# Sink scores of four head pairs in four 32-column tiles, one exp per block, and sink values spread by a mask product

## The chip, the core and the metric

The program runs on one NeuronCore of a Trainium2 chip. The core has five engines with instruction queues of their own: TensorE (PE, matrix products, with weight loads listed apart as PEld), VectorE (DVE), ScalarE (ACT), GpSimd (POOL) and SyncE (SP, used here only to issue transfers). Matrix products land in PSUM, eight banks of 128 partitions; everything else lives in SBUF. The metric is the device time of one execution in microseconds (us). Lower is better.

## What is computed

Attention with a sliding window and sink tokens, followed by a two-layer MLP. There are 4 batches, 8 heads, 768 tokens and a head dimension of 64.

```python
keep = (pos_k < 4) | ((pos_q - pos_k >= 0) & (pos_q - pos_k < 128))
a = softmax(where(keep, q @ k.T / 8, -1e9))
x = (a @ v).transpose(0, 2, 1, 3).reshape(3072, 512)
h = x @ w_in                          # 512 -> 2048
out = (h * sigmoid(1.702 * h)) @ w_out   # 2048 -> 512
```

So each query sees the 128 tokens up to its own, and the first four tokens of its batch: the sinks. For queries in the first 256 tokens of a batch the kernel treats the sinks with the window itself. For all later queries the sinks are scored apart.

## The kernel before

Work is cut into 12 blocks of 256 tokens, three for each batch (`NK = B * R`; the block is `k`, its batch `b`, its place in the batch `r`). The eight heads are handled as four pairs `p`; two heads of 64 fill 128 partitions. For every block the kernel does this:

- **load** (L375): q, k and v of the block come from memory as float32, by SP (two of block 0 by ACT). GpSimd, VectorE or ScalarE cast them to float16 (`copy`, L277-278; every cast has that line).
- **turn** (L472): q and k are transposed to `blkT`, by PE for the first four blocks (`turn_on_pe`, transposes at L507, the permutation `perm` as second operand) and by a transposing DMA for the rest.
- **sink keys and values**, only for the first block of a batch. GpSimd copies the four sink keys out of the transposed block into `ks16` (L493). It is a matrix of 128 columns for each pair, zero outside the sink columns. GpSimd copies the sink values into `vs16` (L455) in four small copies. Both tensors are set to zero once, at the start, on GpSimd (L329, L330).
- **front** (L537), for blocks with `r > 0`, once for each pair: one 128x128 product of the sink keys with the 256 queries (L547) into a bank of PSUM, and one exp on ScalarE into `ats` (L555). With 8 such blocks these are 32 products and 32 exps. Only 8 of the 128 output rows of a pair belong to sinks; the rest multiply zero rows of `vs16` later.
- **scores** (L559): window scores for one pair or two, in products of 64 rows of the array each, the two heads of a pair in the two halves (L589), exp on ScalarE (L609), and from block 2 on a mask product on VectorE (L616). Blocks 0 and 1 add the mask as a bias on PE instead (L582).
- **back** (L627): attention times values on PE (L649), sinks among them, a reciprocal (L667), a normalising product (L669) and a transpose to `xT` (L688 on PE for blocks 0 to 2, by DMA later).
- **mm1** (L702) and **mm2** (L734): the MLP, L716 and L745, with tanh on ScalarE (L728) and a product on VectorE (L730) between. The result is scaled and copied to `osb` (L764, L766) and written out (L775). All writes go through SP's queue except the very last, a piece of 64 rows by 128 columns, which goes through ScalarE's.

The order of instructions on each engine isn't written by hand. A planner (`Plan.run`, L68) takes every step as an operation with an assumed duration on its engine, its dependencies, a priority that plays the part of a due time, and what it needs of PSUM (`acq`, seven banks shared by classes such as "k" for sink scores and "s" for window scores). It simulates the engines and lists the operations in the order in which they would start. It also puts products of zeros (`warm`, L823) on PE wherever PE would be idle in the first 12 us of its own clock. What comes out is a fixed order for each engine: an instruction that waits holds up everything behind it on its engine. Weights (`weights`, L342) are issued by GpSimd, in the same queue as its casts and copies.

Of the kernel before, what the change touches and what calls it, by code (L numbers as in the profile page):

```python
# [26 lines left out]
def _build_constants() -> np.ndarray:  # L27

    t = _token_of()
    rel = t[None, :] - t[:, None]  # L30
    return np.concatenate([np.eye(P), rel <= 0, rel > 0], axis=1).astype(np.float16)


class Op:
# [18 lines left out]
class Plan:  # L53
# [4 lines left out]
    def op(self, eng, dur, lat, fn, deps=(), prio=0.0, acq=None, rel=(), kind=""):  # L58
        return self.any({eng: (dur, lat)}, lambda _: fn(), deps, prio, acq, rel, kind)
# [130 lines left out]
def pe_ns(n):  # L190
    return n / 2.4 + 2.5
# [3 lines left out]
def kernel(  # L195
# [34 lines left out]
    def ring(name, n, shape, dt):  # L230
        return [pool.tile(list(shape), dt, name=f"{name}{i}") for i in range(n)]

    const = pool.tile([P, 3 * P], FP16, name="const")
    ident = const[:, 0:P]
    seen = pool.tile([P, 2 * P], FP16, name="seen")
    perm = pool.tile([P, P], FP16, name="perm")
# [4 lines left out]
    w_out16 = pool.tile([P, NF, d_model], FP16, name="w_out16")  # L241
    blkT = ring("blkT", RB, (P, 2, NP, 2, P), FP16)
    vs16 = pool.tile([P, B, NP, 2, E], FP16, name="vs16")
    ks16 = pool.tile([P, B * NP, P], FP16, name="ks16")
    qk32 = ring("qk32", RS, (P, 2, H, 2, D), FP32)
    v32 = ring("v32", RS, (P, H, 2, D), FP32)
    qk16 = ring("qk16", RQ, (P, 2, 2, H, D), FP16)
    v16 = ring("v16", RV, (P, 2, H, E), FP16)
    at = ring("at", RA, (P, 2, 512), FP16)
    ats = ring("ats", RA, (P, TB), FP16)  # L250
    rcp = ring("rcp", RR, (P, 2, 2), FP32)
    xn = ring("xn", RR, (P, 2, 2, D), FP16)
    xb = ring("xb", 2, (P, 2, NP, 2, D), FP16)
# [34 lines left out]


    NEVER = -1e9  # L290
    o_zero = op("DVE", 100, 200, lambda: nc.vector.memset(zero, 0.0), prio=NEVER, kind="const")  # L291
    o_ident = op("POOL", 700, (300, 8), lambda: nc.gpsimd.dma_start(const, const_d.ap()), prio=NEVER - 1, kind="load")

# [18 lines left out]
    def biases():  # L312
# [13 lines left out]
    o_perm = op("POOL", 330, 450, lambda: nc.gpsimd.tensor_copy(  # L326
        out=perm.rearrange("r (h g) -> r h g", h=NP), in_=ident.rearrange("r (g h) -> r h g", h=NP)),
        [o_ident], prio=NEVER, kind="const")
    o_vs0 = op("POOL", 2200, 2300, lambda: nc.gpsimd.memset(vs16, 0.0), prio=NEVER + 3, kind="const")  # L329
    o_ks0 = op("POOL", 2200, 2300, lambda: nc.gpsimd.memset(ks16, 0.0), prio=NEVER + 2, kind="const")  # L330
    o_table = op("ACT", 1300, 1400, lambda: nc.scalar.activation(out=dummy, in_=zero[:, 0:8], func=AF.Exp),
                 [o_zero], prio=NEVER + 8, kind="const")

# [41 lines left out]
    def load(k):  # L375
# [74 lines left out]
                o_cv[k, p] = got  # L450
        if r == 0:
            def f():
                for t in range(2):
                    for i in range(2):
                        nc.gpsimd.tensor_copy(  # L455
                            out=vs16[64 * t + 32 * i : 64 * t + 32 * i + 2, b, :, i],
                            in_=w16[64 * t : 64 * t + 2, 0, i::2],
                        )
            o_vs[b] = op("POOL", 1400, 1500, f, [*o_cv[k, 0], *o_cv[k, NP - 1], o_vs0], prio=nominal(k - 1, 0), kind="vs")
            uses("v16", k % RV, o_vs[b])  # L460

    k_ap = k

# [8 lines left out]
    def turn(k):  # L472

        b, r = divmod(k, R)
        h8 = L / 8
        base = attend(k, 0)
        c16, T = qk16[k % RQ], blkT[k % RB]
        war = reuse("blkT", k % RB)
        o_t = []
        if k < KT:  # L480
            for i in range(2):
                for e in range(2):
                    o_t.append(turn_on_pe(k, e, i, T, eights(c16)[:, e, i], war))
        else:
            o_t.append(turn_by_dma(k, T, slots(c16), war))
        for p in range(NP):
            o_qkT[k, p] = [o[p] for o in o_t]
        o_t = list({id(o): o for x in o_t for o in x}.values())
        if r == 0:
            def ks():  # L490
                for i in range(2):
                    d = slice(64 * i, 64 * i + 64)
                    nc.gpsimd.tensor_copy(  # L493
                        out=ks16[d, NP * b : NP * b + NP].rearrange("d p (i a) -> d p i a", i=2)[:, :, :, 32 * i : 32 * i + 2],
                        in_=T[d, 1, :, 0].rearrange("d p (i a) -> d p i a", i=2)[:, :, :, 0:2],
                    )
            o = op("POOL", 500, 640, ks, o_t + [o_ks0], prio=base - 4 * h8, kind="ks")
            uses("blkT", k % RB, o)
            for p in range(NP):
                o_ks[b, p] = o  # L500
# [33 lines left out]
        uses("qk16", k % RQ, o)  # L534
        return [o] * NP

    def front(k, p):  # L537

        b, r = divmod(k, R)
        u = NP * k + p  # L540
        base = attend(k, 2 * p)
        h8 = L / 8
        Q = turned(k, p, 0)
        As = ats[u % RA]
        if r:
            def sk():
                nc.tensor.matmul(  # L547
                    f32(o_k)[:, 0:TB], ks16[:, NP * b + p], Q.rearrange("d j s -> d (j s)"),
                    start=True, stop=True,
                )  # L550
            war = reuse("ats", u % RA)
            o_k = op("PE", pe_ns(TB), TB / 2.4 + 166, sk, o_qkT[k, p] + [o_ks[b, p]] + war, prio=base - 3.1 * h8,
                     acq=("k", 1), kind="sink")
            hold(k, p, o_k)
            o_se[k, p] = op("ACT", TB / 1.2 + 50, TB / 1.2 + 170, lambda: nc.scalar.activation(  # L555
                out=As, in_=f32(o_k)[:, 0:TB], func=AF.Exp, scale=scale),
                [o_k] + war, prio=base - 2.6 * h8, rel=[(o_k, 0)], kind="exps")

    def scores(k, pairs):  # L559

# [66 lines left out]
    def back(k, p):  # L627
# [2 lines left out]
        u = NP * k + p  # L630
        base = attend(k, 2 * p)
        h8 = L / 8
        A, As = at[u % RA], ats[u % RA]
        vt, vp = v16[k % RV], v16[(k - 1) % RV]

        def avp():
# [12 lines left out]
                        nc.tensor.matmul(avp()[:, j, i], a_, v_, start=(n == 0), stop=(n == len(mms) - 1))  # L649

        dur = 12 * 31 if r else 6 * 31
        deps = [*o_m[k, p], *o_cv[k, p]] + ([o_se[k, p], *o_cv[k - 1, p], o_vs[b]] if r else [])
        rc, X = rcp[u % RR], xn[u % RR]
        if k < KX:
            war = reuse("xn", u % RR)
# [5 lines left out]
        o_a = op("PE", dur, dur + 166, av, deps + war, prio=base - 1.5 * h8, acq=("a", 1), kind="av")  # L661
        uses("at", u % RA, o_a)
        if r:
            uses("ats", u % RA, o_a)
            uses("v16", (k - 1) % RV, o_a)
        uses("v16", k % RV, o_a)
        o_r = op("DVE", 100, 200, lambda: nc.vector.reciprocal(out=rc, in_=avp()[:, :, :, D]),  # L667
# [66 lines left out]
    def mm2(k):  # L734
        b, r = divmod(k, R)
        g = gT[k % RG]
        for j, c0, c1 in ((0, 0, 512), (1, 0, 512)) if k < NK - 1 else ((0, 0, 512), (1, 0, 384), (1, 384, 512)):
            w = c1 - c0
            last = w < d_model
            holder = []  # L740
            prev = None
            for s in range(NS):
                def f(s=s, j=j, holder=holder, c0=c0, c1=c1, w=w):
                    for Fi in (2 * s, 2 * s + 1):
                        nc.tensor.matmul(  # L745
                            f32(holder[0])[:, 0:w], g[:, Fi, bass.ts(j, P)], w_out16[:, Fi, c0:c1],
                            start=(Fi == 0), stop=(Fi == NF - 1),
                        )
                deps = [o_g[k, s], o_w[4 + s // 2]] + ([prev] if prev else [])
                o = op("PE", 2 * pe_ns(w), pe_ns(w) + w / 2.4 + 166, f, deps,  # L750
                       prio=nominal(k + 1, 4 * j + s / 2) + 3 + c0 / 100 * L, acq=None if s else ("o", 1), kind="mm2")
                uses("gT", k % RG, o)
                holder.append(o)
                prev = o
            if not c0:
                oi = n_o[0] % RO
                n_o[0] += 1
                war = reuse("osb", oi)
            O = osb[oi]
            row = k * TB + j * P  # L760

            def f(e, O=O, holder=holder, c0=c0, c1=c1, w=w):
                if e == "ACT":
                    nc.scalar.mul(O[:, c0:c1], f32(holder[0])[:, 0:w], 0.5)  # L764
                else:
                    nc.vector.tensor_scalar_mul(O[:, c0:c1], f32(holder[0])[:, 0:w], 0.5)  # L766

            prio = nominal(k + 1, 4 * j + 4) + 4
            e = "DVE" if c0 else "ACT"
            o_c = [op(e, w / 1.2 + 50, w / 1.2 + 170, lambda f=f, e=e: f(e), [holder[-1]] + war, prio=prio,  # L770
                      rel=[(holder[0], 0)], kind="oc")]
            for i in range(2):
                eng = "ACT" if c0 and i else "SP"
                def f(O=O, i=i, row=row, c0=c0, c1=c1, dma=nc.scalar if eng == "ACT" else nc.sync):
                    dma.dma_start(  # L775
                        out[row : row + P, c0:c1].rearrange("(p i) f -> i p f", i=2)[i], O[64 * i : 64 * i + 64, c0:c1]
                    )
                o_d = op(eng, 590, (420, 4), f, o_c, prio=prio, kind="out")
                uses("osb", oi, o_d)
# [3 lines left out]
    for k_ in range(NK):  # L783
        load(k_)
        turn(k_)
        for p_ in range(NP):
            front(k_, p_)
        for ps_ in [(0,), (1,), (2,), (3,)] if k_ < PAIRED_FROM else [(0, 1), (2, 3)]:
            scores(k_, ps_)
        for p_ in range(NP):  # L790
            back(k_, p_)
        if k_ >= 1:
            mm1(k_ - 1)
        if k_ >= 2:
            mm2(k_ - 2)
# [79 lines left out]
```

## Time and profile before

Four runs took 224.36 to 225.09 us, with a median of 224.85 us. The profiled execution took 224.98 us, of which the instructions span 223.0 us.

| engine | busy, us | share of the span | instructions |
|---|---|---|---|
| PE | 217.7 | 98% | 2186 |
| ACT | 132.9 | 60% | 263 |
| DVE | 125.0 | 56% | 272 |
| POOL | 90.7 | 41% | 158 |

A matrix product's listed duration includes its way through the array, during which the next one already runs: 768 products at L716 have a mean of 273 ns, while eight of them in a row take 0.87 us on the chain of waits, or 109 ns each. So the space that a product takes on PE is read from the chain or from the starts of neighbours, not from its mean duration. The granted clock of PE is full in all of the span.

### The profile page before, as it was taken

To read this page: it belongs to the slowest core of one execution; us is meant where nothing else is said; L and a number is where in the kernel's file an instruction comes from. 1 tells how busy PE (TensorE), PEld (TensorE's weight loads), DVE (VectorE), ACT (ScalarE), POOL (GpSimd) and SP (SyncE) were. 2 spreads that over 40 slices of the span, in tenths; PEclk is the share of its full clock that TensorE was granted. 3 is DMA by queue.
4 is the path that set the end of the run, shared out by engine and by line. 5 is a ranking of instruction groups with operands and counts; after the bars stand their busy time and mean duration, and the time that the engine had idled before them with its cause. 6 is when DMAs were issued, how large, how long until landed. Compare 5 with 4: busy or idle time off the path is not lost.

```text
span 223.0 us, 5479 instructions
## 1 busy us (share of the span) xinstructions
PE 217.7 (98%) x2186; PEld 154.3 (69%) x2186; DVE 125.0 (56%) x272; ACT 132.9 (60%) x263; POOL 90.7 (41%) x158
## 2 busy tenths in 40 slices
PE   8999999999999999999999999999999999999993
PEld 8968977667757766766676667767667676666652
DVE  1675865588727765665555665575465655634310
ACT  3298555776557776565486577555577486444320
POOL 8299013578991785703815917507500000000000
PEclk9999999999999999999999999999999999999999
DMA  5999999999789989299599589399541212231224
GB/s 203 342 155 200 197 257 249 344 288 265 158 122 215 247 161 310 50 166 259 114 210 247 72 193 255 74 205 243 104 92 43 61 36 47 51 69 25 50 47 94
DMA packets 65864, 36.36 MB, mean 163 GB/s; under 512 B 27792, under 2 KB 60832, under 8 KB 65840
## 3 DMA queue, kind: packets, MB, share of 16 engines
q1 hardware_dynamic: 61200, 31.17, 59.1%
q0 software_dynamic: 4272, 4.29, 11.9%
q10 hardware_dynamic: 368, 0.56, 0.8%
q8 instruction: 17, 0.28, 0.5%
q14 instruction: 7, 0.06, 0.1%
HBM read 27.36 MB, written 6.29 MB: 151 GB/s over the span
## 4 chain that ended last, share of the span: by engine, by line
PE 93%; ACT 3%; DMA 1%; DVE 1%; issue 0%; SPq 0%; ACTq 0%
PE bank L716 38%; PE bank L745 35%; PE bank L649 6%; PE bank L589 5%; PE bank L823 4%; PE bank L547 2%; ACT at L609 1%; PE bank L507 1%; DMA out_dram<-osb 1%; PE bank L688 1%; PE bank L582 1%; ACT blkT L278 0%; DVE gT L730 0%; ACT osb L764 0%; ACT th L728 0%
## 5 line engine op out<-in xcount | busy, mean ns | idle before, releaser
L745 PE MATMUL bank<-w_out,gT 128*128 128x512 f16 (+2 forms) x400 | 100.2, 370 | 0.0
L716 PE MATMUL bank<-xT,w_in 128*128 128x256 f16 x768 | 100.1, 273 | 0.0
L730 DVE SCALAR_TENSOR_TENSOR gT<-th,bank 128x512 f16<-128x512 f16 x96 | 65.8, 685 | 48.5 <-ACT th L728 47.7
L716 PEld LDWEIGHTS <-w_in 128*128 128x128 f16 x768 | 72.9, 98 | 22.6 <-issue 2.5
L728 ACT ACTIVATE th<-bank 128x512 f16<-128x512 f32 x96 | 57.8, 602 | 46.1 <-PE bank L716 45.2
L278 POOL CAST qk<-qk 64x512 f16<-64x512 f32 (+1 forms) x73 | 44.3, 609 | 54.6 <-DMA qk<-in_q_dram 34.4
L609 ACT ACTIVATE at<-bank 128x512 f16<-128x512 f32 (+1 forms) x96 | 50.3, 571 | 14.7 <-PE bank L589 14.4
L745 PEld LDWEIGHTS <-gT 128*128 128x128 f16 x400 | 36.4, 98 | 21.9 <-issue 0.3
L616 DVE TENSOR_TENSOR at<-at,bank 128x1024 f16<-128x1024 f16 (+1 forms) x40 | 25.6, 640 | 20.7 <-ACT at L609 20.5
L278 POOL CAST v<-v 64x512 f16<-64x512 f32 x45 | 27.6, 614 | 6.4 <-DMA v<-in_v_dram 4.1
L649 PE MATMUL bank<-v,at 128*128 128x65 f16 x352 | 21.2, 193 | 0.2 <-DVE v L278 0.2
L764 ACT ACTIVATE osb<-bank 128x512 f32<-128x512 f32 (+1 forms) x24 | 14.4, 598 | 10.6 <-PE bank L745 10.6
L649 PEld LDWEIGHTS <-at 128*128 128x128 f16 x352 | 17.6, 98 | 4.0 <-issue 0.3
L555 ACT ACTIVATE ats<-bank 128x256 f16<-128x256 f32 x32 | 12.6, 394 | 7.1 <-PE bank L547 7.0
L669 DVE TENSOR_TENSOR xb<-bank,rcp 128x256 f16<-128x256 f32 x36 | 15.2, 421 | 0.5
L649 PE MATMUL bank<-vs,ats 128*128 128x65 f16 x128 | 14.8, 193 | 0.0
L667 DVE RECIPROCAL rcp<-bank 128x4 f32<-128x4 f32 x48 | 8.6, 179 | 9.5 <-PE bank L649 8.4
L649 PEld LDWEIGHTS <-ats 128*128 128x128 f16 x128 | 11.9, 97 | 2.2 <-ACT th L728 0.2
L589 PE MATMUL bank<-blkT 64*128 64x256 f16 x192 | 13.4, 244 | 0.0
L589 PEld LDWEIGHTS <-blkT 64*128 64x128 f16 x256 | 8.0, 94 | 7.7 <-issue 6.7
L823 PE MATMUL bank<-zero 128*128 128x128 f16 x99 | 8.6, 265 | 1.0 <-DVE zero L291 1.0
L547 PE MATMUL bank<-blkT,ks 128*128 128x256 f16 x32 | 8.7, 272 | 0.1
(41 smaller groups left out, 86.7 us busy)
## 6 DMA issues: line engine op xcount, KB each, us to landing
v<-in_v_dram SPq DMA_DIRECT2D x12, 512.0 KB, 7.0
out_dram<-osb SPq DMA_DIRECT2D x46, 128.0 KB, 2.7
qk<-in_q_dram SPq DMA_DIRECT2D x8, 512.0 KB, 5.1
qk<-in_k_dram SPq DMA_DIRECT2D x8, 512.0 KB, 6.1
qk<-in_q_dram SPq DMA_DIRECT2D x8, 256.0 KB, 5.1
w_in<-in_moe_w_in_dram POOLq DMA_DIRECT2D x4, 512.0 KB, 6.9
w_out<-in_moe_w_out_dram POOLq DMA_DIRECT2D x4, 512.0 KB, 14.4
qk<-in_k_dram SPq DMA_DIRECT2D x6, 256.0 KB, 5.5
```

The source lines that it names most:

```text
L278: {"POOL": nc.gpsimd.tensor_copy, "DVE": nc.vector.tensor_copy, "ACT": nc.scalar.copy}[e](out=out, in_=in_)
L589: nc.tensor.matmul(f32(o_s, 2 * n + i)[:, c : c + w], src[d, j], Q[d].rearrange("d j s -> d (j s)")[:, q0 : q0 + w], start=k >= KM, stop=T ...
L609: nc.scalar.activation(out=A[:, i, 0:W], in_=f32(o_s, 2 * n + i)[:, 0:W], func=AF.Exp, scale=scale)
L616: nc.vector.tensor_tensor(out=A[:, :, 0:W], in0=A[:, :, 0:W], in1=mask[:, c0 : c0 + W].unsqueeze(1).to_broadcast((P, 2, W)), op=ALU.mult,)
L649: nc.tensor.matmul(avp()[:, j, i], a_, v_, start=(n == 0), stop=(n == len(mms) - 1))
L669: o_n = op("DVE", 300, 425, lambda: nc.vector.tensor_tensor(out=X, in0=avp()[:, :, :, 0:D], in1=rc.to_broadcast((P, 2, 2, D)), op=ALU.mult ...
L716: nc.tensor.matmul(f32(holder[0])[:, bass.ts(e, TB)], w_in16[:, c, bass.ts(Fi, P)], X[:, c] if k < KX else X2[:, :, c], start=(c == 0), st ...
L728: o_t = op("ACT", 477, 600, lambda first=first: nc.scalar.activation(out=th[first.places[0]], in_=f32(first), func=AF.Tanh, scale=0.851), ...
L730: o_g[k, s] = op("DVE", 565, 690, lambda first=first, s=s: nc.vector.scalar_tensor_tensor(out=g[:, 2 * s : 2 * s + 2].rearrange("p a t -> ...
L745: nc.tensor.matmul(f32(holder[0])[:, 0:w], g[:, Fi, bass.ts(j, P)], w_out16[:, Fi, c0:c1], start=(Fi == 0), stop=(Fi == NF - 1),)
L764: nc.scalar.mul(O[:, c0:c1], f32(holder[0])[:, 0:w], 0.5)
L823: nc.tensor.matmul(warm_bank[:, 0:P], zero, zero, start=True, stop=True)
```

## The change

- **Sink keys.** `ks16` gets 32 columns for each pair instead of 128: head 0 of the pair has its four sinks in columns 0 to 3, head 1 in columns 16 to 19. Clearing it is a quarter of the work.
- **Sink scores.** `front` runs once for each block with `r > 0`, instead of once for each pair. It issues four products, one for each pair, with 128 rows and 32 columns of the array each; pair `p` writes partitions 32p to 32p+31 of one bank. One exp over 128 x 256 follows, into one of three buffers `ats` instead of six. The planner is given 297 ns on PE for the four.
- **Sink values.** Four DMAs on SP's queue, one for each sink token, read the sink values of all batches and heads straight from `v` into a float32 tensor `vs32`, each head at its own partitions (16 times the head, plus the sink's place). VectorE clears `vs32` at the start and sets its column of ones. For each batch one product on GpSimd of `vs32` with a 0/1 mask of 128 x 8 writes the whole of `vs16`. That product also writes the zeros, so clearing `vs16` on GpSimd is gone. The mask rides with the constants, which get 8 columns more.
- **Writes.** In the last block, both second halves of the last 128 rows go through ScalarE's queue, instead of only the final one.

```diff
+    row = np.arange(P)
+    sink = (row[:, None] // 16 == np.arange(8)[None, :]) & (row[:, None] % 16 < 4)
...
-    const = pool.tile([P, 3 * P], FP16, name="const")
+    const = pool.tile([P, 3 * P + 8], FP16, name="const")
...
-    ks16 = pool.tile([P, B * NP, P], FP16, name="ks16")
+    ks16 = pool.tile([P, B, NP, 32], FP16, name="ks16")
+    vs32 = pool.tile([P, B, E], FP32, name="vs32")
...
-    ats = ring("ats", RA, (P, TB), FP16)
+    ats = ring("ats", 3, (P, TB), FP16)
...
-    o_vs0 = op("POOL", 2200, 2300, lambda: nc.gpsimd.memset(vs16, 0.0), prio=NEVER + 3, kind="const")
-    o_ks0 = op("POOL", 2200, 2300, lambda: nc.gpsimd.memset(ks16, 0.0), prio=NEVER + 2, kind="const")
+    def no_sinks():
+        nc.vector.memset(vs32, 0.0)
+        nc.vector.memset(vs32[:, :, D : D + 1], 1.0)
+    o_vs0 = op("DVE", 250, 350, no_sinks, prio=NEVER + 1, kind="const")
+    o_vl = []
+    for s_ in range(n_sink):
+        def f(s_=s_):
+            row = 2 * (s_ % 2) + s_ // 2
+            return nc.sync.dma_start(
+                vs32[row::16, :, 0:D], v[:, :, s_, :].rearrange("b h d -> h b d")
+            )
+        o_vl.append(op("SP", 450, (100, 3), f, [o_vs0], prio=VS_AT + s_, kind="loadv"))
+        o_vl[-1].begin = 6200.0
+    o_ks0 = op("POOL", 550, 650, lambda: nc.gpsimd.memset(ks16, 0.0), prio=NEVER + 2, kind="const")
...
             def f():
-                for t in range(2):
-                    for i in range(2):
-                        nc.gpsimd.tensor_copy(
-                            out=vs16[64 * t + 32 * i : 64 * t + 32 * i + 2, b, :, i],
-                            in_=w16[64 * t : 64 * t + 2, 0, i::2],
-                        )
-            o_vs[b] = op("POOL", 1400, 1500, f, [*o_cv[k, 0], *o_cv[k, NP - 1], o_vs0], prio=nominal(k - 1, 0), kind="vs")
+                nc.gpsimd.tensor_tensor(
+                    out=vs16[:, b].rearrange("r p i e -> r (p i) e"), in0=vs32[:, b].unsqueeze(1).to_broadcast((P, H, E)),
+                    in1=const[:, 3 * P : 3 * P + H].unsqueeze(2).to_broadcast((P, H, E)), op=ALU.mult,
+                )
+            o_vs[b] = op("POOL", 1100, 1200, f, [*o_vl, o_ident], prio=nominal(k - 1, 0), kind="vs")
...
-    def front(k, p):
+    def front(k):
...
+        def sk():
+            for p in range(NP):
                 nc.tensor.matmul(
-                    f32(o_k)[:, 0:TB], ks16[:, NP * b + p], Q.rearrange("d j s -> d (j s)"),
+                    f32(o_k)[32 * p : 32 * p + 32, 0:TB], ks16[:, b, p], turned(k, p, 0).rearrange("d j s -> d (j s)"),
                     start=True, stop=True,
                 )
...
+        o_k = op("PE", TB / 2.4 + 190, TB / 2.4 + 260, sk, deps + war, prio=base - 3.1 * h8, acq=("k", 1), kind="sink")
+        hold(k, 0, o_k)
+        o_se[k] = op("ACT", TB / 1.2 + 50, TB / 1.2 + 170, lambda: nc.scalar.activation(
+            out=As, in_=f32(o_k)[:, 0:TB], func=AF.Exp, scale=scale),
+            [o_k] + war, prio=base - 2.6 * h8, rel=[(o_k, 0)], kind="exps")
...
-                eng = "ACT" if c0 and i else "SP"
+                eng = "ACT" if i and k == NK - 1 and j else "SP"
...
-        for p_ in range(NP):
-            front(k_, p_)
+        if k_ % R:
+            front(k_)
```

The four tiled products and the exp stand in for the 32 products and exps of before. The products of attention with values still take 128 rows of `ats` and `vs16`.

## The prediction

> **What bounds the kernel now.** I read the shares of busy time first, then the chain of waits cut into stretches, because a share of 98% says nothing of where the other 2% lie. The chain from 16.3 to 216 us is summed up in the first line below, the chain from the start to 16.3 us in the second:
>
> ```profile
> by line: PE bank L716 42.9%; PE bank L745 39.4%; PE bank L649 7.2%; PE bank L589 5.4%; PE bank L547 1.8%; PE bank L507 0.9%; PE bank L688 0.9%; PE bank L582 0.7%; DVE gT L730 0.4%; ACT th L728 0.3%; ACT osb L764 0.3%; issue 0.1%; ACTq L728
> by line: PE bank L823 49.8%; ACT at L609 18.8%; ACT blkT L278 5.9%; PE bank L507 5.5%; DVE xn L669 2.7%; PE bank L310 2.4%; issue 2.3%; ACT ats L555 2.2%; PE bank L582 2.1%; PE bank L589 1.9%; PE bank L688 1.4%; DVE rcp L667 1.1%; DVE zero
> ```
>
> The reader is to see three stages. From 16.3 us on PE carries all but about 1% of the chain: the time there is the sum of what the products take on PE, and work taken off another engine is worth nothing. Before 16.3 us half the chain is zeros (L823), put there by the planner, and then ScalarE leads with exps and copies. Behind the last product (219.2 us) lies a tail of 3.8 us: a copy, writes and their landing.
>
> Three kinds of numbers decide the change on PE: what a sink product takes, what a change of the array's tiling costs, and how well tiles overlap. The chain around 65 us, and the starts of PE's products there, show all three (columns: start, length or time from the first start to the last end, both in us):
>
> ```profile
> 65.23 0.11 PE bank L547
> 65.34 0.55 PE bank L589 x12
> 65.89 0.54 PE bank L745 x2
> 66.43 0.11 PE bank L547
> ...
> 65.07 0.27 PE L547 MATMUL bank<-blkT,ks 128*128 128x256 f16 x1
> 65.27 0.23 PE L589 MATMUL bank<-blkT,blkT 64*128 64x128 f16 x2
> 65.34 0.33 PE L589 MATMUL bank<-blkT 64*128 64x256 f16 x4
> 65.50 0.22 PE L589 MATMUL bank<-blkT,blkT 64*128 64x128 f16 x2
> 65.56 0.33 PE L589 MATMUL bank<-blkT 64*128 64x256 f16 x4
> 65.82 0.60 PE L745 MATMUL bank<-w_out,gT 128*128 128x512 f16 x2
> ```
>
> A sink product (L547) takes 0.11 us of PE. The 12 products of L589 are of 64 rows, two to a step. Their second pair starts 0.23 us after the first pair, although each half of the array then has 512 columns to stream, which a row of L745 products takes 0.216 us for (four in 0.86 us): the two halves do run together, and products of neighbouring tiles start within about 10 ns (two of them span 0.23 us at a mean of 0.226). But the group starts 0.20 us after L547 where 0.11 was due, and L745 starts 0.32 us after the last pair where 0.23 was due: about 0.09 us on the way into the tiling and 0.09 to 0.11 on the way back (after another group eight L716 take 0.98 us instead of 0.87).
>
> **The sinks on PE.** Removed: 32 x 0.109 = 3.5 us, 0.436 us for each of 8 blocks. Added for each block: into 32-column tiles 0.09, one stream of 256 columns 0.109, three later starts, and back 0.11. No row shows column tiles. Bounds: if they overlap as the row tiles do, three starts are 0.03 us and a block costs 0.34; if they run one after another it is 0.09 + 0.436 + 0.11 = 0.64; if the group stands next to a scores group, which is due right after it by its priority, one of the two changes is shared and it is 0.25. I take the row tiles as nearest and half the blocks adjacent: 0.34 and 0.25 alternate, 0.295 on average. 8 x (0.436 - 0.295) = 1.1 us. I take off 0.3 us because four weight loads of 32 columns follow the change into the tiling at once: **0.8 us** gained, ends -1.6 (all serial) and +1.5 (all adjacent).
>
> The Trainium skill speaks on both sides here. "TensorE: Matmul & The Clock Gate", Part 3 (Packing small matmuls), gives a packed group the time of one product plus about 4 ns for each further tile; that alone would make a block 0.12 us and the gain 8 x 0.316 = 2.5 us. "TensorEngine Tiling (Array Packing)" says under Key Properties that a change of the tiling mode drains the array, and under Restrictions that column tiling switches the fast weight load off. The 0.2 us there and back at 65 us is this case's number for such a drain, and it eats two thirds of the 2.5 us. I keep the row's price.
>
> **The exps.** 24 of 32 go: 24 x 0.39 = 9.4 us of ScalarE. From 16.3 us on they lie beside PE, at nothing. Of the three saved in block 1 (17.07, 18.81, 21.46 us in ScalarE's timeline) none is on the chain; only the first (15.14) is, and it stays. Nothing gained. The join adds a wait: the exp of pair 0 now waits for the keys of all four pairs. In block 1 and later one copy or one DMA carries all pairs, so they are ready together; nothing lost. The stall near 41 us, where the chain leaves PE for 1.4 us (tanh, then the product at L730), lies between PE's products and costs no more than about 0.2 us of them; its cover may move either way.
>
> **GpSimd and the start.** Clearing `ks16` falls from 1.83 us to a quarter, 0.46; clearing `vs16` (1.85 us) goes; VectorE clears 260 floats at about 1.2 us, where it is idle until 4.92. GpSimd's queue in the start of before:
>
> ```profile
> 1.91 1.83 POOL L330 MEMSET ks<- 128x2048 f16 x1
> 3.65 1.85 POOL L329 MEMSET vs<- 128x2080 f16 x1
> 5.56 0.29 POOL L326 COPY perm<-const 128x128 f16<-128x128 f16 x1
> ...
> 10.78 0.56 POOL L493 COPY ks<-blkT 64x16 f16<-64x16 f16 x2 [2.34 <-DVE blkT L278]
> 11.33 1.48 POOL L349 DMA_DIRECT2D w_in<-in_moe_w_in_dram  x2
> 12.85 0.71 POOL L278 CAST v<-v 64x512 f16<-64x512 f32 x1
> 13.63 1.94 POOL L455 COPY vs<-v 2x260 f16<-2x260 f16 x4
> ```
>
> `perm` is an operand of the first transposes (L507, 8.49 us on PE). It can now run when its constants land, 4.92 us by VectorE's wait, 0.64 us earlier. The trace shows the casts of block 0 done at 7.08 us, while PE stands in 21 products of zeros until 8.5: the transposes come late because the planner's order puts zeros ahead of them, and `perm` behind 4.4 us of clearing in the planner's own figures is the likeliest reason. If the order moves, L507 can start up to 8.49 - 7.15 = 1.3 us earlier, and the copies, the sink keys (10.78), the first weights (11.33) and the exps follow. But block 0's values hold the next step: L649 at 14.45 waits for their casts, and the first MLP product (19.01) waits for `xT`, ready at 18.6. Ends: nothing, and 1.2 us. I take **0.4 us**, nearer the lower end, since only the transposes of q clearly had `perm` as their last input.
>
> **Sink values.** The four copies (1.94 us, later 1.77) become one product over 520 elements with two inputs. No row shows GpSimd with two inputs; the nearest, a cast of 512 elements, takes 0.61 us, so at least 0.6. The upper end is what it replaces. "GPSIMD Engine Reference", 3.1, gives 2.6 cycles an element; 520 of them at its 1.2 GHz make an estimate of 1.1 us. All lie beside PE. The new wait is for the four DMAs. They stand in SP's queue behind v, whose issues end at 6.27; at some 0.6 us each they end near 8.7, and nothing else is in that queue until 25.19, so they delay no one. What they wait for in memory is the traffic ahead. From 10 to 20 us, in slices of 0.25 us, it was:
>
> ```profile
> GB/s 301 297 301 293 291 289 334 113 35 0 0 45 16 37 53 143 221 209 205 209 205 197 221 209 193 209 205 209 197 221 201 213 205 209 250 176 172 193 205 193
> ```
>
> The queue runs dry at 12 us, so 32 KB more should land by 12.5 or 13, and the product can stand where the copies stood, 13.63. Its first user is at 21.75. Cost nothing. If that cover goes, the casts of v and the third piece of `w_in` (issued 16.19) wait behind it in GpSimd's queue.
>
> **The tail.** SP issues its last four writes from 218.85 on, each about 0.56 us, the last at 220.0, landing in 2.0. ScalarE's single one is issued at 219.53 and lands in 2.3. With one write moved to ScalarE, both queues issue their last at 219.53; the end moves from 222.0 to 221.83 at most, **0.2 us**.
>
> **Sum.** 0.8 + 0.4 + 0.2 = 1.4 us, against the profiled execution: 224.98 - 1.4 = **223.6 us**. The profiled execution lies 0.13 above the median of 224.85, so the gain read against the median is 1.25 us, 0.6%.
>
> **Rivals.**
> - *The start moves in full.* The 1.2 us come instead of 0.4: 222.8 us. For it: PE's zeros before 8.5 us are pure waiting. Against it: v's casts and `xT` come next.
> - *No change.* The tiles drain on both sides in every block and the loads are exposed (0.4 us a block), and the start is held by v: 0.3 + 0 + 0.2 gives 224.5; with a little lost in the new order, 224.8. For it: 98% on PE, and only 3.5 us of it touched.
> - *Slower, the tiles run one after another.* Then each block pays four products and two drains, 0.64 against 0.436: +1.6, less the tail's 0.2: 226.4 us. It decides from 0.44 us a block on. For it: no row shows column tiles, and their weight loads may be slow. Against it: the halves of L589 overlap.
> - *Slower, GpSimd's queue stands still.* If the sink values land as late as v's slowest load (11.9 us after issue, about 20 us), the weights behind come some 6 us late, of which about 3 are covered: 227 us. Against it: the dry queue at 12 us.
> - That the change does not do what it says would show as 32 sink products; the code leaves no room for it.
>
> **How the numbers follow.** Forecast 0.45, with its own range 222.9 to 224.2; start in full 0.15; no change 0.18; tiles in series 0.16; GpSimd's queue 0.06. The range 222.3 to 226.0 leaves out most of the last two. A measurement of this kernel can tell 0.3% (0.67 us) from no change: faster 0.58 (the first two, but for a small part of the forecast's upper end), same 0.20, slower 0.22.
>
> **What would show it.** On PE, eight groups of four products of 32 columns with starts some 10 ns apart, and 0.25 to 0.4 us from the product before a group to the one after, less that product; starts 0.1 us apart or more would prove the serial rival. L507 before 8.2 us and the first L716 before 18.7 show the start's step. GpSimd's product at L455's place, with no wait for a DMA, shows the cover. The last write in SP's queue issued near 219.5 less the gain shows the tail. The prediction is wrong if PE's chain has gaps in the middle which before hasn't, for the new order is not to be read from this profile.

## The result, and the profile after

The changed kernel takes a median of **223.59 us** (43 runs, 222.65 to 226.56), the kernel before 224.69 us in the same series (64 runs, 223.89 to 225.55). The ratio is 0.9953, with a 95% interval from 0.9939 to 0.9966: 1.1 us faster. The forecast was 223.6 us. Seven of the 43 runs lie near 226.5 us, where the kernel before has none; the ratio does not count them, they turn out to be the change's own doing (last part of the experiments), and with them the mean over all runs falls by 0.6 us only (224.68 to 224.08).

The profiled execution of the changed kernel took 224.32 us and spans 222.5 us. Its page gives these busy times:

```profile
PE 216.6 (97%) x2186; PEld 150.7 (68%) x2186; DVE 125.2 (56%) x274; ACT 125.8 (57%) x239; POOL 85.5 (38%) x145
```

ScalarE lost 7 us of work and GpSimd 5 us; whether any of that reaches the span is for the experiments to tell. What PE won does not show in its busy time either, since that counts each product's way through the array. It shows in the starts. Two groups of sink products of the changed kernel, each with PE's neighbours in time (start, length, both in us):

```profile
65.66 0.81 PE L760 MATMUL bank<-w_out,gT 128*128 128x512 f16 x3
66.40 0.29 PE L561 MATMUL bank<-blkT,ks 128*32 128x256 f16 x4
66.62 0.23 PE L604 MATMUL bank<-blkT,blkT 64*128 64x128 f16 x2
...
108.50 0.59 PE L760 MATMUL bank<-w_out,gT 128*128 128x512 f16 x2
109.03 0.29 PE L561 MATMUL bank<-blkT,ks 128*32 128x256 f16 x4
109.25 1.05 PE L731 MATMUL bank<-xT,w_in 128*128 128x256 f16 x8
```

Four products span 0.29 us, at 0.283 us for one: they start 2 to 3 ns apart and run together. The group at 109.03 was due at 108.93 (two L760 of 0.216 us from 108.50 on), and the next product starts at 109.25: 0.32 us for the block, where four whole products took 0.436. At 66.40 a scores group follows at once, and the way out of one tiling is the way into the other. There are seven groups of the first kind and one of the second.

The start looks as if it had moved by 0.66 us. These are PE's products of zeros and the first transposes, before the change (first three lines) and after it:

```profile
0.99 6.16 PE L823 MATMUL bank<-zero 128*128 128x128 f16 x64 [0.99 <-DVE zero L291]
7.38 1.33 PE L823 MATMUL bank<-zero 128*128 128x128 f16 x21
8.55 0.61 PE L507 MATMUL bank<-perm,qk 128*128 128x128 f16 x8
```

```profile
0.99 5.51 PE L838 MATMUL bank<-zero 128*128 128x128 f16 x64 [0.99 <-DVE zero L295]
6.72 1.34 PE L838 MATMUL bank<-zero 128*128 128x128 f16 x21
7.89 0.61 PE L522 MATMUL bank<-perm,qk 128*128 128x128 f16 x8
```

The same 64 and 21 zeros stand ahead of the transposes. The only difference is that the 64 took 5.51 us instead of 6.16. The zeros in slices of 1 us, before (first two lines) and after (slice, its length, then busy time and number of products on PE, of loads on PEld, granted clock, transfers' share, GB/s):

```profile
4.00:5.00 1.00, 1.00 (x12) 1.00 (x10) 1.00 1.04 395
5.00:6.00 1.00, 1.00 (x13) 1.00 (x11) 1.00 1.09 408
```

```profile
4.00:5.00 1.00, 1.00 (x15) 1.00 (x13) 1.00 1.07 412
5.00:6.00 1.00, 1.00 (x22) 1.00 (x20) 1.00 1.05 402
```

PE begins at half its pace: the zeros start 107 ns apart until 5.97 us before the change and until 4.59 us after it, and 56 ns apart from there on. The listed clock of 1.00 doesn't show this, because the trace's first record of the clock begins only about there. So the full clock that was read for the whole span of the kernel before is not shown for its first 6 us. GpSimd's queue in the changed kernel:

```profile
1.92 0.55 POOL L348 MEMSET ks<- 128x512 f16 x1
5.16 0.35 POOL L330 COPY perm<-const 128x128 f16<-128x128 f16 x1 [2.69 <-DMA const<-const]
...
13.10 0.61 POOL L281 CAST v<-v 64x512 f16<-64x512 f32 x1 [0.19 <-DMA v<-in_v_dram]
...
13.85 1.05 POOL L471 TENSOR_TENSOR vs<-vs,const 128x520 f16<-128x520 f32 x1
```

`perm` is ready at 5.5 us, some 2.4 us before PE gets to it. The product that spreads the sink values takes 1.05 us and waits for no transfer.

### The profile page after: what moved, and what is told of

The parts are those of the page before. It is cut to its first block, busy times and chain, and to the rows that moved or that the text cites. A ratio compares the mean times of both kernels' runs of the same rounds, so it can differ in the third digit from the quotient of the medians.

```text
span 222.5 us, 5455 instructions
## 1 busy us (share of the span) xinstructions
PE 216.6 (97%) x2186; PEld 150.7 (68%) x2186; DVE 125.2 (56%) x274; ACT 125.8 (57%) x239; POOL 85.5 (38%) x145
## 4 chain that ended last, share of the span: by engine, by line
PE 82%; DMA 12%; SPq 2%; POOL 2%; issue 0%; ACT 0%; DVE 0%; POOLq 0%
PE bank L760 36%; PE bank L731 34%; DMA w_out<-in_moe_w_out_dram 7%; PE bank L664 6%; PE bank L604 5%; DMA v<-in_v_dram 3%; SPq L407 2%; DMA out_dram<-osb 1%; PE bank L522 1%; PE bank L561 1%; POOL w_in L367 1%; POOL vs L471 0%; POOL w_out L367 0%; PE bank L703 0%; ACT osb L779 0%
## 5 line engine op out<-in xcount | busy, mean ns | idle before, releaser
L760 PE MATMUL bank<-w_out,gT 128*128 128x512 f16 (+2 forms) x400 | 99.2, 370 | 0.7 <-DMA w_out<-in_moe_w_out_dram 0.6
L624 ACT ACTIVATE at<-bank 128x512 f16<-128x512 f32 (+1 forms) x96 | 48.6, 570 | 14.4 <-PE bank L604 14.2
L760 PEld LDWEIGHTS <-gT 128*128 128x128 f16 x400 | 36.4, 98 | 24.1 <-issue 1.5
L838 PE MATMUL bank<-zero 128*128 128x128 f16 x99 | 8.0, 252 | 1.0 <-DVE zero L295 1.0
L281 ACT COPY blkT<-bank 128x512 f16<-128x512 f16 (+1 forms) x12 | 5.7, 510 | 4.5 <-PE bank L522 4.4
L838 PEld LDWEIGHTS <-zero 128*128 128x128 f16 x99 | 7.4, 116 | 1.0 <-DVE zero L295 1.0
```

Of the source, the lines that this page charges most:

```text
L281: {"POOL": nc.gpsimd.tensor_copy, "DVE": nc.vector.tensor_copy, "ACT": nc.scalar.copy}[e](out=out, in_=in_)
L624: nc.scalar.activation(out=A[:, i, 0:W], in_=f32(o_s, 2 * n + i)[:, 0:W], func=AF.Exp, scale=scale)
L760: nc.tensor.matmul(f32(holder[0])[:, 0:w], g[:, Fi, bass.ts(j, P)], w_out16[:, Fi, c0:c1], start=(Fi == 0), stop=(Fi == NF - 1),)
L838: nc.tensor.matmul(warm_bank[:, 0:P], zero, zero, start=True, stop=True)
```

## The experiments

All ratios are to the kernel before, run on the same chip. There are three series, each on a chip of its own: c0, e1, e3 and e4; e2, e5, e6 and e7; c1, e8, e9 and e10. The times given with them are medians of all runs.

### The changed kernel again (c0_repeat)

> The changed kernel once more, as the measure for the others on the same chip. Both theories: 223.6 us, 1.1 below the kernel before. Its profile should show again 64, 21, 3 and 11 products of zeros ahead of block 0's steps. If the first 64 take another time than 5.5 us (they took 6.16 us before the change), then the earlier start of the transposes in the changed kernel's profile was not the change's doing but the array's own warming.

Measured: 223.42 us, 22 runs, ratio 0.9950 (0.9935 to 0.9964). The zeros are 64, 21, 3 and 11 again, and the 64 took 5.71 us. In the fourteen profiles the same 64 products took between 5.14 and 6.60 us, and where all zeros are kept, what stands behind them on PE moved along. All of them show the two paces, 107 and 56 ns; the change of pace comes between 3.95 and 7.04 us, and that makes the difference. The kernel before was profiled once, so its usual time is not known, but 6.16 us lies well within this range. So the start's 0.66 us comes from the moment at which the array reached its full pace in that execution, and no reordering by the change is behind it. This profile has no wait for `w_out`, which the first one had (0.65 us at 33.38 us).

### The tiles alone undone (e1_full_array)

```diff
-                    f32(o_k)[32 * p : 32 * p + 32, 0:TB], ks16[:, b, p], ...
-                    start=True, stop=True,
+                    f32(o_k)[:, 0:TB], ks16[:, b, P * p : P * p + P], ...
+                    start=p == 0, stop=p == NP - 1,
```

`ks16` becomes wide enough that each pair's 128 columns hold its keys in columns 32p on and zeros elsewhere; the four products add up in the bank. Clearing the wider `ks16` takes GpSimd 2.25 us instead of 0.55, but still ends before the constants land.

> The four sink products of a block are made with 128 columns each on the whole array again, added up in one bank; the exp, the sink values and the order on every engine stay as in the changed kernel. If the tiles bring the gain: each of 8 blocks takes 0.436 us instead of about 0.32 (0.22 where a scores group follows at once), so 0.9 to 1.1 us slower than the changed kernel, 224.6 us, about the time before the change. If the gain comes from the start, the exps or GpSimd: no slower than the changed kernel, 223.6 us.

Measured: 224.40 us, ratio 0.9987 (0.9969 to 1.0005). By the ratios that is 0.8 us slower than the changed kernel, by the medians 1.0, and it is no longer clear of the kernel before. The trace shows where. The order on PE is the same in both, so the same instructions can be set against each other; here ScalarE's copies of results to `osb`, with the sink groups that lie behind each:

| sink groups passed | c0_repeat, us | e1_full_array, us | lag, us |
|---|---|---|---|
| 2 | 46.81 | 46.96 | 0.15 |
| 3 | 70.54 | 70.90 | 0.36 |
| 4 | 81.96 | 82.43 | 0.47 |
| 5 | 114.65 | 115.23 | 0.58 |
| 6 | 131.63 | 132.32 | 0.69 |
| 7 | 164.32 | 165.12 | 0.80 |
| 8 | 181.31 | 182.21 | 0.90 |

Each group adds about 0.11 us, and 0.21 where a scores group stands next to it (the third). Between the groups nothing is lost or won. The tiles are the gain: 0.9 us in the traces.

### Sink values alone (e2_values_only)

```diff
-    o_vs0 = op("POOL", 2200, 2300, lambda: nc.gpsimd.memset(vs16, 0.0), ...
+        o_vl.append(op("SP", 450, (100, 3), f, [o_vs0], prio=NEVER + 15.0 + s_, kind="loadv"))
...
+                nc.gpsimd.tensor_tensor(
+                    out=vs16[:, b], in0=vs32[:, b].unsqueeze(2).to_broadcast((P, NP, 2, E)),
```

> The kernel before with the sink values alone taken from the change: four DMAs into a float32 tensor, the mask product on GpSimd, no clearing of vs16 on GpSimd; 32 sink products of 128 columns, 32 exps and the writes as before. The prediction's start step says that perm comes early and the transposes with it: 0.4 us faster than the kernel before, 224.3 us, with fewer than 21 products of zeros ahead of the first transposes. If the transposes are held by the planned zeros and not by perm: 21 zeros again, and the time of the kernel before within 0.2 us, 224.7 us.

Measured: 224.44 us, 12 runs, ratio 1.0030 (0.9998 to 1.0063). Seven runs are at 224.0 to 224.4, five at 226.5 to 227.0; this ratio counts the five. `perm` is ready at 5.3 us, and twenty-one zeros stand ahead of the first transposes again. So an early `perm` moves nothing. The sink values by themselves do not make the kernel faster by an amount that these runs could tell, and they are enough to bring the runs near 226.5 us. The profile fell among the five; it is read below.

### Four exps in place of one (e5_four_exps, e8_four_exps_planned)

```diff
+            for p in range(NP):
+                got = nc.scalar.activation(
+                    out=As[32 * p : 32 * p + 32], in_=f32(o_k)[32 * p : 32 * p + 32, 0:TB], func=AF.Exp, scale=scale)
```

> The changed kernel with four exps for a block, one for each pair on its 32 partitions, in place of one; the order on all engines stays. ScalarE gets 24 x 0.38 = 9.2 us of work back. If exps lie beside PE at nothing, as predicted: 223.4 us, as the repeat of the changed kernel, within 0.2 us. If ScalarE's relief is a part of the gain, above all in block 1 where the exps of the scores follow: 0.4 to 1 us slower, 224.0 us or more.

Measured: 225.13 us, ratio 1.0023 (1.0001 to 1.0045). The expectation of no cost fell: by the ratios this is 1.6 us slower than c0_repeat, which ran on another chip. In the traces the same copies as above lag by 0.46 us at 64 us, by 1.42 at 70.5 us, and by no more after that. Block 4 lies between; ScalarE, VectorE and PE there in e5_four_exps:

```profile
66.16 1.54 ACT L572 ACTIVATE ats<-bank 32x256 f16<-32x256 f32 x4 [1.37 <-PE bank L561]
67.72 2.07 ACT L629 ACTIVATE at<-bank 128x512 f16<-128x512 f32 x4
...
68.83 0.69 DVE L636 TENSOR_TENSOR at<-at,bank 128x1024 f16<-128x1024 f16 x1 [4.19 <-ACT at L629]
...
69.58 0.23 PE L669 MATMUL bank<-v,at 128*128 128x65 f16 x2 [0.62 <-DVE at L636]
```

The four small exps stand together ahead of the scores' exps, so these start 1.56 us after the first sink exp, where it is 0.31 us in c0_repeat; the mask product comes later, and PE waits for it with the block's first product of values.

This could have been the planner's order alone, made for one exp. So the second kernel tells the planner the full duration:

```diff
-        o_se[k] = op("ACT", TB / 1.2 + 50, TB / 1.2 + 170, se,
+        o_se[k] = op("ACT", NP * (TB / 1.2 + 50), NP * (TB / 1.2 + 50) + 120, se,
```

> Four exps for a block as in the last series, but with their full duration told to the planner, so that the order allows for them. If ScalarE's work itself costs nothing and only an order made for one exp let PE wait (0.97 us in block 4): 223.6 us, within 0.3 us of the changed kernel. If the four exps in a row ahead of the scores' exps hold PE whatever the order, so that the single exp is a part of the gain: 224.3 us or more, with PE waiting for the mask product or the scores' exps near block 4 again.

Measured: 224.36 us, ratio 0.9993 (0.9970 to 1.0017), where c1_repeat has 0.9948. The two intervals overlap, so the size rests on the traces. Against c1_repeat, whose start had the same waits, the copies lag by 0.16 us at 67 us, by 0.70 at 73.7 and by 0.93 at the end, so about 0.8 us is lost behind the start. PE's wait in block 4 is still there, though listed with 0.2 us only. In both orders that were tried, four exps in a row cost PE time: about 1 us behind 64 us with the first, 0.8 us with the second. In the kernel before they did not stand in a row: each stood ahead of its own pair's scores. So the one exp is not shown to be a gain of its own over the kernel before, but once the sinks of four pairs are joined, it is what keeps the join free.

### The tail (e7_tail)

```diff
-                eng = "ACT" if i and k == NK - 1 and j else "SP"
+                eng = "ACT" if c0 and i else "SP"
```

> The changed kernel with the writes of the last block as before: three of the last four on SP's queue, one on ScalarE's. Predicted from the tail step: SP's last write is issued some 0.5 us after VectorE's last copy instead of at once, and the end of the span lies 0.1 to 0.2 us further behind that copy (3.5 us instead of 3.4). The rival: ScalarE's longer issue and landing eat it, no difference.

Measured: 223.57 us, ratio 0.9952 (0.9928 to 0.9975): too little for the times to tell from 0.9950. The traces tell it. From the start of VectorE's last copy to the end of the span it is 3.95 us here (217.75 to 221.7), 3.80 before the change (219.20 to 223.0) and 4.05 in e2_values_only (220.75 to 224.8), the three profiles with the old writes. In the changed kernel it is 3.68 and 3.72 (218.82 to 222.5, 217.78 to 221.5), and in no profile with the new writes more than 3.77. So the writes are worth about 0.2 us, give or take 0.1.

### The start without zeros (e6_few_zeros)

```diff
-    order = plan.run(warm=warm, warm_until=12000.0, late_bank=12500.0)
+    order = plan.run(warm=warm, warm_until=5000.0, late_bank=12500.0)
```

> The changed kernel without the zeros behind the first 64 (21, 3 and 11 products left out, 2.0 us of PE). If these zeros hold the transposes back: the first transpose starts at about 7.2 us, when block 0's casts are done (7.1), instead of 7.9 to 8.1, and everything until the first MLP product comes 0.5 to 1 us earlier: 222.7 us. If the start is held by the values of block 0 and the weights: the transposes come earlier, but L664's first wait grows, and the first MLP product stays near 19.1: 223.4 us. If the array's clock falls without the zeros: slower, 224 us or more.

Measured: 223.15 us, six runs, ratio 0.9933 (0.9912 to 0.9953), not told apart from 0.9950. The transposes start at 6.82 us. The first MLP products of this kernel with a line of its waits and its product of sink values, then the MLP products of c0_repeat:

```profile
17.97 2.36 PE L731 MATMUL bank<-xT,w_in 128*128 128x256 f16 x20
22.13 1.04 PE L731 MATMUL bank<-xT,w_in 128*128 128x256 f16 x8
...
PE bank L664 <- POOL v L281: 1.0, 1, 1.0
...
15.57 1.06 POOL L471 TENSOR_TENSOR vs<-vs,const 128x520 f16<-128x520 f32 x1 [0.92 <-DMA vs<-in_v_dram]
```

```profile
19.06 2.36 PE L731 MATMUL bank<-xT,w_in 128*128 128x256 f16 x20
22.04 1.04 PE L731 MATMUL bank<-xT,w_in 128*128 128x256 f16 x8
```

The zeros did hold the start: without them the first MLP product comes 1.1 us earlier. But at 22 us the lead is gone. PE then waits 1.0 us for GpSimd to cast block 1's values, which stand behind the weights in GpSimd's queue. That queue is no earlier than in c0_repeat, although PE is, because the product of sink values waits 0.92 us for its transfer; in the profiles of the changed kernel it does not. Both theories had a part of it: the zeros hold the first step, GpSimd's queue the second, and there the new transfers cost something.

### The other sink products held back (e3_hold), or on VectorE (e4_dve)

```diff
+            if b:
+                o_vs[b].begin = nominal(k - 1, 0)
```

> The products that spread the sink values of batches 1 to 3 are held back on GpSimd until their batch is near, so that the last two pieces of w_out are issued near 21 us instead of 23.0; no other engine's order changes. If these three products cause PE's new wait for w_out at 33.4 us (0.65 us): the wait is gone and the time falls by 0.4 to 0.65, to 223.1 us. If the piece that comes late is the one issued at 17.1 us, ahead of the three products: the wait stays, and the time stays within 0.2 us of the changed kernel.

Measured: 223.95 us, ratio 0.9961 (0.9946 to 0.9977). The last pieces of `w_out` were issued at 21.0 us instead of 24.6 in c0_repeat, and nothing was gained. Neither profile has the wait for `w_out`, so the two can't tell which piece was late. The first profile of the changed kernel can: the piece issued at 17.1 us took 16.2 us to land, at 33.3, where PE's wait ended. So it was the earlier piece, as the second reading had it. For e4 the product itself moves too:

```diff
-                nc.gpsimd.tensor_tensor(
+                nc.vector.tensor_tensor(
```

> The products that spread the sink values run on VectorE instead of GpSimd, those of batches 1 to 3 held back to their batch. If GpSimd's product at 13.85 us[...] is what makes the third piece of w_in and all weights behind it land later (23.2 us instead of 22.7, the second piece of w_out 33.3 instead of 31.5): the gap in the traffic at 18 us and the wait for w_out are gone, 223.0 us. If the stream of weights is late for another reason, such as the sharing of the memory traffic: 223.6 us, with the wait still there.

Measured: 224.14 us, ratio 0.9970 (0.9954 to 0.9985). No gain; its interval and c0_repeat's overlap, so a loss isn't shown either. No run of it lies near 226.5 (14 runs, at most 225.24). The wait for `w_out` was not in any other profile of the changed kernel, so why the weights came late in that one execution stays open.

### The runs near 226.5 us (c1_repeat, e9_product_later)

> The changed kernel a third time, as the measure for the two that follow: 223.4 to 223.6 us, with some of its runs near 226.5 us, as in the first two series (7 of 43 and 4 of 22), where the kernel before has none above 225.6.

Measured: ten runs, median 223.77 us, ratio 0.9948 (0.9915 to 0.9980), three of them between 226.15 and 226.48. This time the profile caught such a run (226.45 us). VectorE's and GpSimd's casts of v, the product, PE's wait, and from the table by windows the stretch that follows (busy time of each engine, then granted clock, transfers' share, GB/s):

```profile
12.83 3.02 DVE L281 CAST v<-v 64x512 f16<-64x512 f32 x3
13.02 1.45 POOL L281 CAST v<-v 64x512 f16<-64x512 f32 x2
14.52 1.05 POOL L471 TENSOR_TENSOR vs<-vs,const 128x520 f16<-128x520 f32 x1
...
L281 DVE CAST v<-v x3: 413/721/1847, 12.8 to 14.0; 64x512 f16<-64x512 f32 x3
...
15.91 0.43 PE L664 MATMUL bank<-v,at 128*128 128x65 f16 x9 [1.54 <-DVE v L281]
...
16.30:19.80 3.50, 3.50 (x44) 2.84 (x42) 2.55 (x11) 1.47 (x3) 3.40 (x6) 0.55 1.21 178
```

The same engines in c0_repeat:

```profile
12.23 1.61 DVE L281 CAST v<-v 64x512 f16<-64x512 f32 x3
12.41 0.70 POOL L281 CAST v<-v 64x512 f16<-64x512 f32 x1
14.83 0.61 POOL L281 CAST v<-v 64x512 f16<-64x512 f32 x1 [1.71 <-DMA v<-in_v_dram]
15.48 1.05 POOL L471 TENSOR_TENSOR vs<-vs,const 128x520 f16<-128x520 f32 x1
```

When block 1's v lands late (14.83), GpSimd has to wait for it, and VectorE finishes its three casts meanwhile. When it has landed already, GpSimd runs cast, cast and product in a row from 13.02 to 15.57, and VectorE's third cast, begun at 14.0, ends only at 15.85: 1.85 us for what takes 0.43. PE waits 1.54 us for it. In e2_values_only and e8_four_exps_planned the same cast took 1.84 and 1.85 us. The profile of e4_dve is the control: there GpSimd has a third cast where the product stood.

```profile
13.12 1.92 DVE L281 CAST v<-v 64x512 f16<-64x512 f32 x3
13.30 2.21 POOL L281 CAST v<-v 64x512 f16<-64x512 f32 x3
...
L281 DVE CAST v<-v x3: 410/724/739, 13.1 to 14.3; 64x512 f16<-64x512 f32 x3
```

VectorE's third cast, begun at 14.3, takes 0.74 us there. So it is the product that holds the cast, and not the row of GpSimd's instructions. The Trainium skill, "SBUF — State Buffer", in SBUF: two separate sides, says that VectorE, in its modes with two ports, and GpSimd share a pair of ports as an exclusive lock: whichever starts first gets it, and the other blocks for the whole instruction. The blocking fits these traces, with the held cast ending 0.3 us after the product in c1, e2 and e8, and 0.3 us after GpSimd's second cast in e4. The order does not: in c1 the product began 0.5 us after VectorE's cast and still went first. Whether the cast runs in such a mode, and why it gets its turn between two casts but not between cast and product, no run here shows.

The first MLP product comes 3.2 us later here than in c0_repeat (22.30 against 19.06). The longer zeros make 0.6 us of this, the wait 1.3 (the first sink group starts at 16.27 instead of 14.38), and 1.3 comes after that, where PE has a granted clock of 0.55. In e8_four_exps_planned the clock falls in the same way. In e2_values_only it stays at 1.00 after a wait of 1.53 us, and its long runs are still 2.4 us above the others. So a long run does not need the fall of the clock, and why it follows the wait in two profiles and not in the third stays open. What decides whether v has landed in time is open too; the three long profiles are those in which PE's pace changed late, at 6.3 to 6.7 us, and in the other profiles with the product at this place it changed at 5.2 us or before.

The remedy tried is one of order only:

```diff
-            o_vs[b] = op("POOL", 1100, 1200, f, [*o_vl, o_ident], prio=nominal(k - 1, 0), kind="vs")
+            o_vs[b] = op("POOL", 1100, 1200, f, [*o_vl, o_ident], prio=nominal(k - 1, 0) if b else 2 * NEVER, kind="vs")
+            if not b:
+                o_vs[b].begin = 15150.0
```

> Only GpSimd's order is changed: batch 0's mask product stands behind the third and fourth piece of w_in, not right behind the casts of v. If the product and VectorE's casts of v shut each other out (a cast of 0.43 us took 1.84 us beside the product, and PE waited 1.5 us for it): no run near 226.5 any more, all of VectorE's casts of v under 0.8 us, a median of 223.0 to 223.3 us. If the slow runs have another cause: still one in five or so near 226.5, median as the changed kernel.

Measured: 223.53 us, 12 runs from 222.70 to 224.36, ratio 0.9949 (0.9931 to 0.9968). The median expected, 223.0 to 223.3, was missed; no run is long. GpSimd goes from the casts to issuing weights, and VectorE's longest cast of v takes 0.72 us in the profile, as in c0_repeat: in this execution, too, GpSimd had to wait for v (1.38 us), so the profile doesn't put the remedy to the test, only the times do. Both changes together:

> The last kernel without the zeros behind the first 64. The start's theories add up: the values of block 0 hold the start, so the time stays within 0.3 us of the last kernel, 222.9 to 223.3 us; if the zeros hold it, 222.5 us.

Measured: 223.16 us, seven runs from 222.64 to 223.96, ratio 0.9935 (0.9909 to 0.9960). That is 0.4 us below e9, within both intervals: in its profile PE still waits 0.5 us for VectorE's cast of v and 0.2 for `w_in`. Of the changed kernel's 75 runs in all three series 14 took 226.1 us or more; of these two kernels' 19 none did. At the changed kernel's rate, e9's 12 runs would be free of long ones by chance in about 1 of 12 cases; with e10's seven and e4's 14, the kernels without the product at that place have 33 runs and none long, about 1 in 1000. Of the others that keep it there, e1, e3, e5, e7 and e8 have long runs as well (1 of 14, 4 of 22, 3 of 12, 2 of 10, 2 of 13), and e6 has none in six. None of the three without it is told apart from the changed kernel in the middle, but the tail of long runs is gone.

## Why the prediction was right, and which step was not

- **PE bounds the kernel, and the sinks pay on PE**: right, shown by e1. The drain's price read from the row tiles (0.09 in, 0.11 out) holds for column tiles: 0.32 us a block was measured where 0.34 was taken, 0.22 beside a scores group where 0.25 was. Two terms were off by about 0.3 us each and cancelled, which was luck. One block of eight stands beside a scores group, not half of them; and the 0.3 us taken off for weight loads isn't there, since the four loads lie within the group's 0.29 us. The step's 0.8 us measured 0.8 to 1.0.
- **The skill's two rules**: the one product plus 4 ns for each tile is right for the group itself (0.29 us for four of 0.283), and alone would have given an estimated 2.5 us in all; the change of tiling takes the rest. The sum with both is the one that was measured (7 x 0.32 + 0.22 = 2.46 us in place of 3.49).
- **The start, 0.4 us**: this step failed. It held that `perm` was the last input of the transposes. The profile before already spoke against it: `perm` was ready at 5.85 us there, 2.7 us before the transposes. The runs show the planned zeros ahead of them, 21 as before, so nothing moved (e2, c0), and e6, without these zeros, starts the transposes at 6.82 us. It also shows that even an earlier start is lost by 22 us. The earlier transposes of the first profile after were the luck of one execution.
- **The exps, nothing**: right against the kernel before, but the reason was too wide. A row of four ahead of the scores' exps did not lie beside PE (e5, e8).
- **The sink values, nothing**: this holds for most runs only. In the changed kernel's profiles the product waits for no transfer, as argued, although the four issues took until 11.2 us and not until 8.7; in e6 it waited 0.92 us. The product's 1.05 us is what the estimate said (1.1). The cover was named wrongly: it was to be the casts and weights behind the product, but what suffers is VectorE's cast beside it. No step of the prediction had the product hold another engine. The runs laid to this are nearly 3 us longer than the rest (14 of 75, one of them profiled).
- **The tail, 0.2 us**: about 0.2 in the traces, unseen in the times.

So 0.9 + 0 + 0.2 makes the 1.1 us that was measured outside the long runs. The sum of 1.4 was 0.3 too high, by the start. That 223.6 was met to the digit is luck: it was counted from an execution of 224.98 us, which lies 0.3 above the median of the longer series.

## What to carry to other kernels

Joining small products in tiles of the array pays one stream plus two changes of tiling (0.2 us here); count those from any tiled group that the kernel already has, and put tiled groups next to each other. When a step on GpSimd is made one larger instruction, ask what VectorE runs at that moment: beside the four small copies of before, VectorE's third cast took 0.53 us. Before an earlier start in a trace is put down to an edit, check that something ahead of it has changed in the order, not only in duration.

## What was not expected of the hardware

- VectorE's cast of 64x512 from float32 took 1.85 us instead of 0.43 beside a GpSimd cast followed by the product, in three profiles (c1, e2, e8). Beside GpSimd's casts alone it took up to 0.74 us, even with three of them in a row (e4).
- After PE had stood for 1.54 us, its granted clock was 0.55 in the next 3.5 us in c1_repeat, and much the same in e8. After 1.53 us in e2 it was 1.00.
- The same 64 products of zeros at the very start took 5.14 to 6.60 us from one execution to the next. They start 107 ns apart, then 56, and the moment of the change differs by 3 us, while the page lists a clock of 1.00 throughout. What comes behind them in PE's queue moves with them.
